# Linear attention with a token mixer: v loaded as bf16 by GpSimd-queue transfers, its products on VectorE, some relus on GpSimd

## The chip, the cores and the metric

The kernel runs on one core of one Trainium2 chip. A core has TensorE (PE, matrix products; PEld is its loading of weights), VectorE (DVE), ScalarE (ACT), GpSimd (POOL) and SyncE (SP, which here only issues transfers), and 16 DMA engines that move data between HBM and the on-chip memory. The metric is the device time of one execution in microseconds (us). Before the change the median of 2 runs is 120.28 us (120.14 to 120.42).

## What is computed

First cosine-weighted linear attention over batch 8, 8 heads, 576 positions, head size 64, then a token mixer over the 512 channels. All inputs and the output are fp32.

```python
theta = np.pi / 2.0 * pos / S
phi(x) = concatenate([relu(x) * cos(theta), relu(x) * sin(theta)])   # on the head axis
kv  = einsum('bhsf,bhsd->bhfd', phi(k), v)
z   = sum over s of phi(k)
num = einsum('bhsf,bhfd->bhsd', phi(q), kv)
den = einsum('bhsf,bhf->bhs', phi(q), z) + 1e-06
x   = num / den                                  # to (batch, seq, 512)
W_tok = scale * einsum('bsd,btd->bst', x @ w_q, x @ w_k)
mixed = einsum('bst,btd->bsd', W_tok, x)
out   = relu(mixed) @ w_out
```

## The kernel before, in words

The work on attention goes in 16 half batches H = 0 to 15: four heads each, that is two pairs of heads, and a pair's data is a tile of 128 partitions by 576 (a "part", a or b). A whole half batch of q, k or v is 128 x 1152. The second stage, the mixer, goes batch by batch, and the last products (WO) in 36 row tiles.

The order of all work is written out by hand in the string ORDER (lines 26 to 67). Each word is one step: a kind, a number, an optional part a or b, a PSUM place after a colon, and an engine after @ (A for ScalarE, V for VectorE, G for GpSimd). Line 555 runs through the words and issues each; every engine then takes its own instructions in just that order and waits for the semaphores that the data needs. So a step that waits holds up all that stands behind it on its engine. Transfers, too, wait in the queue of the engine that issues them until their buffer is free.

The steps that matter here:

- LQ, LK, LV (function load, line 142): transfers of q, k, v into fp32 buffers, one per part of 288 KB, all issued by SP (line 145). There are five buffers each of q, k and v (NRAW, line 101).
- RQ, RK (lines 222 to 227, helper relu at 201): relu of q and k into bf16, on ACT (line 203) or on DVE or POOL (line 205).
- CV (line 229): casts v to bf16 into one of two buffers vb; VS (line 232) then multiplies the bf16 v by the cosine and sine table vtab on DVE (line 234), which gives v2, twice as large.
- VG (line 239): the same product straight from the fp32 v, on POOL (line 248). Before the change the half batches 2a, 3, 4, 6, 7, 8, 13, 14 and 15 go this way; 0, 1, 2b, 5, 9, 10, 11 and 12 go by CV and VS.
- KV (line 268): PE products of k with v2 (lines 275 and 285), copied out of PSUM by KE.
- QT (line 290): PE transposes of q; QM (line 310) multiplies them by the q table on DVE (lines 316 and 320). N (line 329, matmuls at 340) is the product with kv; EP, RC and X divide by the denominator on ACT and DVE (X is line 393).
- XT, XR, XE, WK, KW, WQ, QW, KX, XK, XA, XB, MX, ME: transposes of x and the mixer. XA and XB, copies across partitions, are POOL's and ACT's.
- WO (line 504, matmuls at 509), OE (copy out of PSUM), ST (the stores, issued by SP at line 519, from 16 buffers).

At the start TK and TQ (lines 161 and 174) make index tables with iota on POOL; TV and TW turn them into sine and cosine on ACT.

Of the kernel before, what the change touches and what calls it, by code (L numbers as in the profile page):

```python
# [12 lines left out]
FP32 = mybir.dt.float32  # L13
BF16 = mybir.dt.bfloat16
# [17 lines left out]
XR1:0 RQ3a@A LQ5a X4 QT3:2 RK3@A LK4b VG4b QM3 XT2:6 LV5b XE1@A KV3:4 LV5a XE2@V RQ5b@A LK5a WK0:0
KE3@V RQ4@G LK5b KW0@A N6:4 CW0@A LV6b N7:6 VG4a EP6@A KX0:0 EP7@V RK4a@A LQ7a RJ3 X7 WQ0:1 RQ5a@A
LW2 QT4:2 X6 XK0@A LQ7b RK4b@A QM4 XT3:4 QW0@A CV5b@G LV6a KV4:0 XE3@A CV5a@G LK6b VS5 LV7a QT5:2
KE4@A WK1:4 XB0@A LK6a RK5@G N8:0 QM5 KW1@A N9:6 LQ6b EP8@A MX3:4 ME3@A LV7b VG6b KV5:2 RC8 EP9@V
XA0@A X8 LQ6a WQ1:4 RC9 KE5@A LK7b X9 RQ7@A N11:2 LK7a QW1@V N10:0 VG6a RC11 MX1:6 X11 KX1:4 LW4
ME1@A RC10 LW3 XK1@A MX0:2 X10 XT4:6 RK6b@A LW5 QT7:4 CW2@A XE4@V XA1@G XB1@A XR5:0 LQ8a RK6a@G
RQ6b@A QM7 MX6:6 ME6@A VG7a LQ8b KV6:4 ME0@A XE5@V LV8a MX5:6 MX7:2 RQ6a@V ME5@A LV9b WK2:0 ME7@A
KE6@V QT6:6 LV8b VG7b RK7@A KW2@V MX2:2 LQ9b MX4:4 QM6 KX2:1 LV9a ME4@A WQ2:0 ME2@A LV11a N12:4
CW3@V CW5@A N13:6 CW4@G LQ9a XK2@A KV7:2 EP13@V XA2@G RC12 RC13 X12 LK8a WO6:1 KE7@A QW2@A X13 VG8a  # L40
LK8b N14:4 OE6:0@A N15:2 LK9a EP14@V RQ8@A XR6:6 EP15@V RC14 WO1:1 X14 LV10a XB2@A RC15 WO4:0 LK9b
VG8b X15 CV9@A LV10b QT8:4 RQ9b@V WO7:2 OE4:1@V XE6@A WO3:3 QM8 RQ9a@G LV13b OE7:2@A LK11b MX9:6
MX11:4 ME9@A WO0:0 LQ10a VS9 LQ10b OE3:3@A MX10:6 LV11b ME11@A WO8:2 RK9a@G ME10@A LQ11a RK8@V QT9:4
OE8:4@A OE0:5@V RK9b@G LQ11b KV8:6 OE1:6@A QM9 KV9:2 CV10@G LQ13a KE8@A MX8:6 KE9@A N16:4 LK12a
ME8@A XR7:0 EP16@V RC16 N18:2 VS10 XE7@A WO12:6 LK11a WO10:7 LK10a X16 OE12:7@A LK10b WK3:6 OE10:8@V
CV11@G LV12a N17:4 KW3@A EP18@V N19:0 EP17@V LV12b WQ3:6 EP19@V RC17 RJ9 RK11b@G KX3:7 X17 LQ12a
QW3@A RQ10@A RQ11@G WO11:6 X19 X18 XT8:4 OE11:9@A LQ15b QT10:0 LQ14b VS11a XE8@A XT9:2 LQ12b QM10
WO5:6 RK10a@G LQ13b XE9@A LK13b QT11:0 VS11b XK3@A WO2:4 LK14b XB3@A XA3@G QM11 OE5:10@A RK10b@G
WK4:7 LQ15a OE2:11@A MX14:0 KW4@A LV13a KV10:2 RK11a@V ME14@A CV12@V KV11:6 LK12b KE10@A VS12 ST6
MX13:2 MX12:0 ME13@A KX4:4 LK13a VG13b ME12@A WQ4:5 LV14a KE11@A N21:2 XK4@A N20:0 EP21@V MX15:6  # L50
LV14b WO9:4 EP20@V RC21 ME15@A RC20 X20 RQ13@G N23:6 OE9:12@A X21 N22:0 QW4@A WO14:4 RQ12@A EP22@V
RK12a@G RC22 EP23@V X22 WO13:5 XB4@G OE14:13@A RC23 VG13a X23 RK13b@A QT12:0 ST14 WO17:4 OE13:0@A
LV15a QM12 RK12b@A LQ14a XR10:6 LK14a OE17:14@A MX18:0 XR11:2 LK15b XE10@V XA4@G ME18@A KV12:4
RK13a@A XE11@V WO16:0 VG14 KE12@A MX19:2 QT13:4 OE16:13@V ME19@A MX16:6 WK5:1 QM13 ME16@A ST16
KV13:2 LV15b KW5@A LK15a MX17:0 N24:6 ME17@A ST5 KX5:4 EP24@V KE13@V RC24 N26:2 XK5@V N25:0 X24
EP26@A RQ15@A XB5@G WO20:4 RQ14@G RC26 EP25@V RC25 WO18:5 X25 RK14b@A RK14a@G X26 N27:6 OE18:13@A
XA5@G WQ5:0 RC27 ST18 VG15 X27 KV14:2 QW5@A ST9 OE20:15@A MX20:0 XR13:6 KE14@A XR12:4 ME20@A XE13@V
QT14:2 XE12@A WO21:0 QM14 QT15:6 OE21:10@A N28:4 MX22:2 QM15 ST21 EP28@A WO15:0 RK15@A ST0 WK6:1
# [12 lines left out]
def kernel(  # L71
# [10 lines left out]
    nc = tc.nc  # L82

    B, NH, S, D = q.shape
    DM = NH * D
    DH = moe_w_q.shape[1]
    P = 128
# [14 lines left out]
    XC = DM // 2  # L102
    EPS_PE = (1, 2, 4, 5, 10, 11, 12, 27)
# [38 lines left out]
    def load(nm, H, part):  # L142
        b, h = divmod(H, 2)
        for r in (0, 1) if part is None else (part,):
            nc.sync.dma_start(raw[nm][H % NRAW][:, r, :], src[nm][b][:, 2 * h + r, :])  # L145
# [83 lines left out]
    def CV(H, ps, eng, part):  # L229
        cast(eng, vb_b[H % NPREP].rearrange(flat)[:, part], raw["v"][H % NRAW][:, part])  # L230

    def VS(H, ps, eng, part):
        n = part.stop - part.start
        V.tensor_mul(  # L234
            v2_b[H % NV2][:, part, :, :, 0:D],
            vb_b[H % NPREP][:, part].unsqueeze(3).to_broadcast([P, n, C, 2, D]),
            vtab.unsqueeze(1).to_broadcast([P, n, C, 2, D]))

    def VG(H, ps, eng, part):
        n = part.stop - part.start  # L240
        dst = v2_b[H % NV2]
        s = raw["v"][H % NRAW].rearrange("p r (c d) -> p r c d", d=D)
# [356 lines left out]
```

## Time and profile before

| | |
|---|---|
| median of 2 runs | 120.28 us |
| the profiled execution | 120.89 us, of which its span (first to last instruction) 119.1 us |
| granted TensorE clock, mean | 0.996 |
| busy PE / DVE / ACT / POOL | 98.2 / 90.0 / 84.6 / 69.6 us |
| moved by the DMA engines | 39.38 MB, 331 GB/s over the span |
| read from HBM / written to it | 29.62 / 9.44 MB |

How to read it: the busy time of an engine is what its instructions took, without the issuing of transfers. The page cuts the span into 40 equal slices of 2.98 us and gives the busy share of each in tenths. The chain that ended last goes back from the last instruction, step by step, to what released it. A group of instructions is a line of the kernel, an engine, an operation and shapes, with its total busy time, the mean duration of one in ns, and the idle time of the engine before them with what ended it. SPq is the queue of transfers that SP issues.

### The profile page before, as it was taken

The page shows a single profiled execution, that of the slowest core. Times are in us where ns is not written, and L with a number is a line of the kernel's source. Part 1 is how long each engine was busy: PE and PEld are TensorE (multiplying, and loading weights), DVE is VectorE, ACT ScalarE, POOL GpSimd, SP SyncE. Part 2 cuts the span into 40 slices and gives each one's busy share as a digit, 9 for nine tenths or more (in the row PEclk, how much of TensorE's full clock was granted, in tenths as well). Part 3 has the DMA queues.
Part 4 walks back from the last instruction along what each step waited for, and adds up shares of the span by engine and source line. Part 5 has one row for each costly group of instructions (what it writes and reads, how often), then busy time and mean ns, then how long its engine had stood idle before and what let it go on. Part 6 is the DMA issues. An engine that isn't in the chain of part 4 may idle for free.

```text
span 119.1 us, 4899 instructions
## 1 busy us (share of the span) xinstructions
PE 98.2 (82%) x2077; PEld 67.3 (57%) x2077; DVE 90.0 (76%) x162; ACT 84.6 (71%) x146; POOL 69.6 (58%) x65
## 2 busy tenths in 40 slices
PE   0030699779889789998999999999999999979970
PEld 0020578658677577553767776566767774634420
DVE  2049789995899997899798995997897988644510
ACT  6932394887987969897766997887579777336150
POOL 7304368599679994998674339987999220020000
PEclk9999999999999999999999999999999999999998
DMA  3999999999999999999999999959844797649974
GB/s 97 345 382 406 395 390 359 390 363 378 352 396 391 390 388 387 370 390 368 368 361 394 336 329 372 385 149 369 262 154 155 299 396 296 244 188 396 357 308 175
DMA packets 20662, 39.38 MB, mean 331 GB/s; under 512 B 3232, under 2 KB 3232, under 8 KB 20640
## 3 DMA queue, kind: packets, MB, share of 16 engines
q1 hardware_dynamic: 20640, 39.07, 90.0%
q8 instruction: 16, 0.26, 0.9%
q14 instruction: 6, 0.05, 0.2%
HBM read 29.62 MB, written 9.44 MB: 328 GB/s over the span
## 4 chain that ended last, share of the span: by engine, by line
PE 49%; DVE 23%; DMA 14%; SPq 3%; issue 3%; ACT 3%; POOL 2%; DVEq 0%; ACTq 0%
PE ps L509 17%; DVE x L393 9%; PE ps L340 8%; DVE qm L316 7%; DMA kraw<-in_k_dram 5%; DMA vraw<-in_v_dram 5%; PE ps L285 5%; PE ps L275 5%; PE ps L489 4%; DMA out_dram<-o 4%; SPq L145 3%; PE ps L295 3%; PE ps L466 2%; PE ps L439 2%; PE ps L452 2%
## 5 line engine op out<-in xcount | busy, mean ns | idle before, releaser
L248 POOL TENSOR_TENSOR v<-vraw,vtab 128x1152 bf16<-128x1152 f32 (+1 forms) x15 | 40.6, 2718 | 7.8 <-DMA vraw<-in_v_dram 4.1
L509 PE MATMUL ps<-wow,mix 128*128 128x512 bf16 x144 | 34.6, 380 | 0.8 <-ACT o L209 0.8
L393 DVE TENSOR_TENSOR x<-ps,rec 128x640 bf16<-128x640 f32 x32 | 25.6, 817 | 0.7
L316 DVE TENSOR_TENSOR qm<-ps,qtab 128x1152 bf16<-128x1152 bf16 x24 | 17.0, 750 | 6.4 <-PE ps L295 6.0
L509 PEld LDWEIGHTS <-mix 128*128 128x128 bf16 x144 | 12.7, 98 | 14.6 <-issue 1.4
L209 ACT COPY o<-ps 128x512 f32<-128x512 f32 x25 | 14.5, 585 | 8.1 <-PE ps L509 6.0
L500 ACT ACTIVATE mix<-ps 128x576 bf16<-128x576 f32 x27 | 17.0, 654 | 3.9 <-PE ps L489 3.6
L340 PE MATMUL ps<-kvs,qm 64*128 64x65 bf16 x640 | 14.3, 193 | 1.1 <-ACT kvs L209 0.5
L340 PEld LDWEIGHTS <-qm 64*128 64x128 bf16 x640 | 12.5, 96 | 4.2 <-issue 3.3
L295 PE MATMUL ps<-ident,rq 128*128 128x128 bf16 x108 | 9.0, 235 | 6.6 <-ACT rq L203 6.5
L203 ACT ACTIVATE rk<-kraw 128x576 bf16<-128x576 f32 (+1 forms) x15 | 11.4, 776 | 2.9 <-DMA kraw<-in_k_dram 2.4
L205 POOL TENSOR_SCALAR rk<-kraw 128x576 bf16<-128x576 f32 (+1 forms) x10 | 10.0, 1007 | 5.3 <-DVE x L393 2.0
L211 POOL TENSOR_SCALAR kx<-kx 64x256 bf16<-64x256 bf16 x11 | 4.4, 399 | 14.3 <-ACT kx L209 13.8
L295 PEld LDWEIGHTS <-rq 128*128 128x128 bf16 x108 | 7.3, 105 | 8.3 <-ACT rq L203 6.5
L203 ACT ACTIVATE rq<-qraw 128x1152 bf16<-128x1152 f32 (+1 forms) x12 | 11.5, 961 | 0.2
L285 PE MATMUL ps<-v,rk 64*64 64x130 bf16 x360 | 7.3, 228 | 4.8 <-POOL rk L205 4.8
L209 ACT COPY xT<-ps 128x1280 bf16<-128x1280 bf16 (+1 forms) x9 | 10.6, 1179 | 0.6 <-PE ps L419 0.5
L234 DVE TENSOR_TENSOR v<-vb,vtab 128x2304 bf16<-128x2304 bf16 (+1 forms) x9 | 10.2, 1147 | 0.7 <-POOL vb L211 0.5
L213 DVE COPY o<-ps 128x512 f32<-128x512 f32 x11 | 7.6, 687 | 4.1 <-PE ps L509 4.0
L275 PE MATMUL ps<-v,rk 64*128 64x260 bf16 x108 | 8.1, 295 | 2.0 <-DVE qm L316 1.5
L205 POOL TENSOR_SCALAR rq<-qraw 128x1152 bf16<-128x1152 f32 (+1 forms) x7 | 6.6, 939 | 5.0 <-DMA qraw<-in_q_dram 4.8
L285 PEld LDWEIGHTS <-rk 64*64 64x64 bf16 x360 | 5.9, 112 | 5.7 <-POOL rk L205 5.0
(66 smaller groups left out, 139.8 us busy)
## 6 DMA issues: line engine op xcount, KB each, us to landing
qraw<-in_q_dram SPq DMA_DIRECT2D x32, 288.0 KB, 5.8
vraw<-in_v_dram SPq DMA_DIRECT2D x32, 288.0 KB, 5.8
kraw<-in_k_dram SPq DMA_DIRECT2D x32, 288.0 KB, 5.9
out_dram<-o SPq DMA_DIRECT2D x36, 256.0 KB, 2.9
wof<-in_moe_w_out_dram SPq DMA_DIRECT2D x4, 256.0 KB, 6.1
wkf<-in_moe_w_k_dram SPq DMA_DIRECT2D x1, 128.0 KB, 7.2
wqf<-in_moe_w_q_dram SPq DMA_DIRECT2D x1, 128.0 KB, 5.9
```

The lines of the kernel that those rows point to most:

```text
L203: A.activation(dst, s, AF.Relu)
L205: eng.tensor_scalar(dst, s, FMAX, 0.0, op0=ALU.min, op1=ALU.max)
L209: A.copy(dst, s)
L248: G.tensor_mul(dst[:, part, :, :, 0:D], s[:, part].unsqueeze(3).to_broadcast([P, n, C, 2, D]), vtab.unsqueeze(1).to_broadcast([P, n, C, 2, ...
L275: nc.tensor.matmul(kv_v[:, r, :], rk_b[H % NPREP][a, 2 * c * D:2 * (c + 1) * D], v2_b[H % NV2][a, :, c, :, 0:D + 1], start=(c == 0), stop= ...
L285: nc.tensor.matmul(kv_v[o, r, :], rk_of(H)[a, pr, c, :], v2_b[H % NV2][a, pr, c, :, 0:D + 1], start=(c == 0), stop=(c == C - 1))
L295: nc.tensor.transpose(qt_v[:, c, :], rq_b[H % NPREP][:, c, :, :], ident)
L316: V.tensor_mul(qm_b[H % NQM][:, :, r, 0:C, :], q_t[:, r].unsqueeze(1).to_broadcast([P, 2, C, H2]), qtab)
L340: nc.tensor.matmul(nv[:, pr, u, :], qm_b[H % NQM][a, s, r, 2 * u:2 * u + 2, :], kv_b[H % 2][a, r, pr if H in KV_WIDE else 0, s, 0:D + 1], ...
L393: V.tensor_tensor(x_b[b % NX][:, :, 4 * h:4 * h + 4, :].rearrange("p u (w r) d -> p r w u d", r=2)[:, r], nv[:, :, :, 0:D], rec(g).to_broa ...
L500: A.activation(dst, s, AF.Relu, scale=scale_moe)
L509: nc.tensor.matmul(o, mix_b[bp % 2][:, m, rt * P:(rt + 1) * P], wow[:, m, :], start=(m == 0), stop=(m == NDM - 1))
```

## The change

- For the half batches 2 to 15 (V_CONV) v is read by transfers that POOL issues on its own queue, from fp32 in HBM straight into bf16 buffers vb. There are now five of these (NVB) instead of two. The even half batches are read with one transfer of both parts, the odd ones part by part.
- Half batches 0 and 1 are read as before, into two fp32 buffers (NRV) instead of five.
- All products VG become VS: 13 of one part (2a, 3a, 3b, 4a, 4b, 6a, 6b, 7a, 7b, 8a, 8b, 13a, 13b) and two of both parts (14, 15) move from POOL to DVE. The casts CV2b, CV9 (ACT), CV5a, CV5b, CV10, CV11 (POOL) and CV12 (DVE) go.
- 15 relus move to POOL: from ACT RQ3a, RQ3b, RQ5a, RQ5b, RQ7, RQ15, RK3, RK7, RK13a, RK13b and RK15; from DVE RQ6a, RQ9b, RK8 and RK11a.
- The places of the other words in ORDER stay. The words LV now say when POOL issues the transfer. The first of them, LV2, stands between TI and TQ, at the place of the former LV2b.

The diff, without the ORDER string (only its first lines, as an example):

```diff
-LQ0a TB TZ LQ0b LV0b TK LV1a TI T2 LV0a TV LV2b TQ LQ1b LK1b LK0b TW LK0a RQ0@A LQ1a QT0:0 LV1b
-CV0a@A LQ2a QM0 LQ2b RQ1b@G LK1a CV1a@V LV2a CV0b@V VS0 RK0b@A LK2b LK2a RK0a@G CV2b@A LV3b RQ1a@G
+LQ0a TB TZ LQ0b LV0b TK LV1a TI T2 LV0a TV LV2 TQ LQ1b LK1b LK0b TW LK0a RQ0@A LQ1a QT0:0 LV1b
+CV0a@A LQ2a QM0 LQ2b RQ1b@G LK1a CV1a@V CV0b@V VS0 RK0b@A LK2b LK2a RK0a@G LV3b RQ1a@G KV0:0 CV1b@V
...
+    NVB = 5
+    NRV = 2
+    V_CONV = (2, 3, 4, 5, 6, 7, 8, 9, 10, 11, 12, 13, 14, 15)
...
-    raw = {nm: bufs(NRAW, [P, 2, HC], FP32, f"{nm}raw") for nm in "kqv"}
+    raw = {nm: bufs(NRV if nm == "v" else NRAW, [P, 2, HC], FP32, f"{nm}raw") for nm in "kqv"}
...
-    vb_b = bufs(NPREP, [P, 2, C, D], BF16, "vb")
+    vb_b = bufs(NVB, [P, 2, C, D], BF16, "vb")
...
     def load(nm, H, part):
         b, h = divmod(H, 2)
+        if nm == "v" and H in V_CONV:
+            ps = slice(0, 2) if part is None else slice(part, part + 1)
+            nc.gpsimd.dma_start(vb_b[H % NVB].rearrange("p r c d -> p r (c d)")[:, ps],
+                                src[nm][b][:, 2 * h + ps.start:2 * h + ps.stop, :])
+            return
         for r in (0, 1) if part is None else (part,):
-            nc.sync.dma_start(raw[nm][H % NRAW][:, r, :], src[nm][b][:, 2 * h + r, :])
+            nc.sync.dma_start(raw[nm][H % len(raw[nm])][:, r, :], src[nm][b][:, 2 * h + r, :])
...
     def VS(H, ps, eng, part):
         n = part.stop - part.start
         V.tensor_mul(
             v2_b[H % NV2][:, part, :, :, 0:D],
-            vb_b[H % NPREP][:, part].unsqueeze(3).to_broadcast([P, n, C, 2, D]),
+            vb_b[H % NVB][:, part].unsqueeze(3).to_broadcast([P, n, C, 2, D]),
             vtab.unsqueeze(1).to_broadcast([P, n, C, 2, D]))
```

More of the change, by code (lines that the diff above doesn't have):

```diff
@@ L32 @@
[L32 to L37, printed above, removed]
@@ new lines @@
+N9:6 LQ6b EP8@A MX3:4 ME3@A LV7b VS6b KV5:2 RC8 EP9@V XA0@A X8 LQ6a WQ1:4 RC9 KE5@A LK7b X9 RQ7@G
+N11:2 LK7a QW1@V N10:0 VS6a RC11 MX1:6 X11 KX1:4 LW4 ME1@A RC10 LW3 XK1@A MX0:2 X10 XT4:6 RK6b@A LW5
+QT7:4 CW2@A XE4@V XA1@G XB1@A XR5:0 LQ8a RK6a@G RQ6b@A QM7 MX6:6 ME6@A VS7a LQ8b KV6:4 ME0@A XE5@V
+LV8 MX5:6 MX7:2 RQ6a@G ME5@A LV9b WK2:0 ME7@A KE6@V QT6:6 VS7b RK7@G KW2@V MX2:2 LQ9b MX4:4 QM6
+KX2:1 LV9a ME4@A WQ2:0 ME2@A LV11a N12:4 CW3@V CW5@A N13:6 CW4@G LQ9a XK2@A KV7:2 EP13@V XA2@G RC12
+RC13 X12 LK8a WO6:1 KE7@A QW2@A X13 VS8a LK8b N14:4 OE6:0@A N15:2 LK9a EP14@V RQ8@A XR6:6 EP15@V
@@ new lines @@
+RC14 WO1:1 X14 LV10 XB2@A RC15 WO4:0 LK9b VS8b X15 QT8:4 RQ9b@G WO7:2 OE4:1@V XE6@A WO3:3 QM8 RQ9a@G
+LV13b OE7:2@A LK11b MX9:6 MX11:4 ME9@A WO0:0 LQ10a VS9 LQ10b OE3:3@A MX10:6 LV11b ME11@A WO8:2
+RK9a@G ME10@A LQ11a RK8@G QT9:4 OE8:4@A OE0:5@V RK9b@G LQ11b KV8:6 OE1:6@A QM9 KV9:2 LQ13a KE8@A
+MX8:6 KE9@A N16:4 LK12a ME8@A XR7:0 EP16@V RC16 N18:2 VS10 XE7@A WO12:6 LK11a WO10:7 LK10a X16
+OE12:7@A LK10b WK3:6 OE10:8@V LV12 N17:4 KW3@A EP18@V N19:0 EP17@V WQ3:6 EP19@V RC17 RJ9 RK11b@G
+KX3:7 X17 LQ12a QW3@A RQ10@A RQ11@G WO11:6 X19 X18 XT8:4 OE11:9@A LQ15b QT10:0 LQ14b VS11a XE8@A
@@ L229, in CV @@
     def CV(H, ps, eng, part):
-        cast(eng, vb_b[H % NPREP].rearrange(flat)[:, part], raw["v"][H % NRAW][:, part])
+        cast(eng, vb_b[H % NVB].rearrange(flat)[:, part], raw["v"][H % NRV][:, part])
     def VS(H, ps, eng, part):
@@ L241, in VG @@
         dst = v2_b[H % NV2]
-        s = raw["v"][H % NRAW].rearrange("p r (c d) -> p r c d", d=D)
+        s = raw["v"][H % NRV].rearrange("p r (c d) -> p r c d", d=D)
         if H in VG_SPLIT:
```

37 lines of the change are left out of this document (15 added, 22 removed).

## The prediction, made before the result was known

> **What bounds the kernel now.** I read the page first: the busy shares, then the 40 slices.
>
> ```profile
> span 119.1 us, 4899 instructions
> PE 98.2 (82%) x2077; PEld 67.3 (57%) x2077; DVE 90.0 (76%) x162; ACT 84.6 (71%) x146; POOL 69.6 (58%) x65
> PE   0030699779889789998999999999999999979970
> DVE  2049789995899997899798995997897988644510
> DMA  3999999999999999999999999959844797649974
> ```
>
> No engine is full over the whole span, but the slices show two regimes. Up to the sixteenth slice (about 48 us) PE has holes while DVE and the DMA engines are nearly full; after it PE is full almost to the end. The busy time by stage gives sizes:
>
> ```profile
> 12.00:32.00 20.00, 16.97 (x410) 14.05 (x412) 17.41 (x28) 14.75 (x26) 14.71 (x10) 1.00 1.05 376
> 32.00:44.00 12.00, 10.27 (x249) 8.38 (x245) 11.16 (x20) 9.91 (x19) 10.93 (x8) 1.00 1.05 388
> 44.00:60.00 16.00, 15.55 (x364) 9.96 (x361) 13.97 (x28) 14.05 (x25) 12.04 (x9) 1.00 1.04 375
> 60.00:80.00 20.00, 19.59 (x400) 13.27 (x400) 17.91 (x35) 16.39 (x29) 13.77 (x12) 1.00 0.93 337
> 80.00:100.00 20.00, 19.95 (x566) 13.80 (x558) 16.81 (x33) 15.70 (x29) 12.52 (x8) 1.00 0.77 275
> ```
>
> The columns after the stretch and its length are PE, PEld, DVE, ACT, POOL (busy us and instructions), the granted clock, the DMA share and GB/s. From 44 us to 100 us PE idles 0.45 + 0.41 + 0.05 = 0.9 us in 56. Whatever PE loses before 44 us is therefore lost for good, and a saving elsewhere after 44 us is worth nothing. Before 44 us, DVE idles only 20 - 17.41 = 2.59 us and 12 - 11.16 = 0.84 us. Last I read the chain that ended last, in the front:
>
> ```profile
> 5.23 5.93 DMA kraw<-in_k_dram
> ...
> 25.24 5.81 DMA vraw<-in_v_dram
> ...
> 31.13 0.67 POOL vb L211
> ...
> 31.83 0.68 POOL vb L211
> ...
> 32.53 1.36 DVE v L234
> 33.89 1.34 DVE qm L316 x2
> ...
> 35.28 1.20 PE ps L275 x18
> ```
>
> Two things bound the front: arriving loads (a k half at 11.2 us, a v half at 31 us), and behind them DVE, which hands its product straight to PE. The question is whether the change lightens the loads or burdens DVE.
>
> **The change part by part.** The durations:
>
> ```profile
> L248 POOL TENSOR_TENSOR v<-vraw,vtab 128x1152 bf16<-128x1152 f32 (+1 forms) x15 | 40.6, 2718 | 7.8 <-DMA vraw<-in_v_dram 4.1
> L234 DVE TENSOR_TENSOR v<-vb,vtab 128x2304 bf16<-128x2304 bf16 x6 | 8.1, 1346 | 0.7 <-POOL vb L211 0.5
> L234 DVE TENSOR_TENSOR v<-vb,vtab 128x1152 bf16<-128x1152 bf16 x3 | 2.2, 749 | 0.0
> L205 DVE TENSOR_SCALAR rq<-qraw 128x576 bf16<-128x576 f32 x2 | 1.5, 741 | 0.0
> L205 DVE TENSOR_SCALAR rk<-kraw 128x1152 bf16<-128x1152 f32 x1 | 1.2, 1220 | 0.0
> L205 DVE TENSOR_SCALAR rk<-kraw 128x576 bf16<-128x576 f32 x1 | 0.4, 448 | 0.0
> L213 DVE CAST vb<-vraw 128x1152 bf16<-128x1152 f32 x1 | 0.8, 751 | 0.0
> L205 POOL TENSOR_SCALAR rk<-kraw 128x1152 bf16<-128x1152 f32 x1 | 1.5, 1501 | 0.9 <-ACT kvs L209 0.9
> L205 POOL TENSOR_SCALAR rk<-kraw 128x576 bf16<-128x576 f32 x9 | 8.5, 952 | 4.4 <-DVE x L393 2.0 <-DMA kraw<-in_k_dram 1.6 <-PE ps L489 0.5
> L205 POOL TENSOR_SCALAR rq<-qraw 128x1152 bf16<-128x1152 f32 x4 | 4.6, 1145 | 0.1
> L205 POOL TENSOR_SCALAR rq<-qraw 128x576 bf16<-128x576 f32 x3 | 2.0, 665 | 4.9 <-DMA qraw<-in_q_dram 4.8
> ```
>
> DVE. The 15 fp32 products of POOL (13 half parts, 2 whole) become bf16 products on DVE: 13 x 0.749 + 2 x 1.346 = 12.43 us. What leaves DVE: two q relus 1.48, k relus 1.22 and 0.45, one cast 0.75, together 3.90 us. Net +8.5 us, from 90.0 to 98.5.
>
> POOL loses 40.6 us of products and four casts (two halves of 0.67 and 0.68 in the chain above, two whole ones of at least twice that: some 4 us), and takes 15 relus: six q halves at 0.665, two whole q at 1.145, four whole k at 1.501, three k halves at 0.952, together 15.1 us. Of its 69.6 us about 40 are left, and 21 transfer issues come (seven whole, fourteen half). ACT loses eleven relus and two casts. I cost that at nothing on the path: after 44 us PE is full and can't gain, and before it the chain above has no relu of ACT in it. If ACT were what holds PE in the front, rival E would show it.
>
> Where the DVE work lands decides. The POOL products by stage:
>
> ```profile
> 12.00:32.00 20.00, 11.84 (x5) 1.00 1.05 376
> 32.00:44.00 12.00, 7.93 (x4) 1.00 1.05 388
> 44.00:60.00 16.00, 6.19 (x3) 1.00 1.04 375
> 60.00:80.00 20.00, 5.49 (x2) 1.00 0.93 337
> 80.00:100.00 20.00, 9.14 (x2) 1.00 0.77 275
> ```
>
> (One of the three in the third row is carried over from the second.) The written order keeps each product at its place, so the new DVE products fall there too. Five in 12 to 32 us: +3.75. Four in 32 to 44: +3.00, less one q relu 0.74. So +6.0 us by 44 us, against 3.43 us of DVE idle. In 44 to 60 us: +1.50 - 0.74 - 1.22 = -0.46. In 60 to 80: +1.50 - 0.45 - 0.75 = +0.30 against 2.09 idle. In 80 to 100: two whole ones, +2.69 against 3.19 idle.
>
> How much of the early idle can the products fill? What it was:
>
> ```profile
> DVE rec L359 <- PE ps L340: 1.7, 4, 0.9
> DVE vb L213 <- DMA vraw<-in_v_dram: 0.9, 1, 0.9
> DVE v L234 <- POOL vb L211: 0.5, 1, 0.5
> ```
>
> If all is filled, the excess is 6.0 - 3.43 = 2.6 us; if none, 6.0. The 0.5 behind POOL's cast is fillable, since that cast goes. The 0.9 stands ahead of the first new product, so it isn't. The waits on PE sit in a loop in which PE itself waits for DVE's x and qm, so they move along with it. I take half: 6.0 - 1.7 = +4.3 us on PE by 44 us. DVE's relief of 0.46 after that lets PE regain at most the 0.45 us that it idles there: -0.4. The late 2.7 us I cost at nothing, because PE there never waits for DVE; if that cover (DVE's lead) is gone, they cost up to 2.7.
>
> The first load. The whole of half batch 2 is now issued from POOL ahead of the iota of the q table, while only one half of it stood in SP's stream ahead of the k half that ends at 11.2 us. The sync queue has one 288 KB transfer less ahead of that k half and the other queue two more: 0.295 MB at 376 GB/s is 0.78 us. It is -0.8 if the new queue has moved nothing by then, +0.8 if it has moved all; I take +0.4. The iota's delay holds ACT's table and the first q relu, but DVE then still waits for loads. Later loads keep their total bytes read from HBM, so I take no gain from the narrower writes.
>
> The issue itself. No POOL transfer is in the trace; the nearest rows are SP's issues and the landing:
>
> ```profile
> L145 SPq DMA_DIRECT2D vraw<-in_v_dram x32: 327/332/1236, 1.6 to 83.0; - x32
> DMA to landing us min/median/max: 3.4/5.8/7.2
> ```
>
> Between 0.33 us and 5.8 us of POOL time each. In 12 to 44 us POOL idles 32 - 14.71 - 10.93 = 6.4 us, loses 19.8 us of products and 1.4 of casts, and takes five q halves, one whole q, one whole k, 6.0 us; that frees 21.5 us for some ten issues, so an issue is hidden up to 2.1 us. I take about 1 us, as it is SP's kind of work nearer to the low end, and so nothing on the path. Each issue also waits until the product five half batches earlier has read its bf16 buffer; behind it on POOL stand the relus and the kx copies. With the issues placed some two half batches ahead of their use that product is long done, and I cost the wait at nothing; without that cover it is rival B. SP loses 28 issues of 0.33 us, so q and k go out earlier, but at a DMA share of 1.05 up to 60 us they only share full engines: nothing, unless the front is bound otherwise. The Trainium skill, page "DMA: Bandwidth & Descriptors", section "Latency and other measured facts", puts the first byte of this kind of transfer at about 1 us, the emission overhead of GpSimd's cores; by it the sum stays as it is. No run here shows it yet.
>
> Sum: +4.3 - 0.4 + 0.4 = +4.3, bounds 2.6 - 0.8 - 0.4 = +1.4 and 6.0 + 0.8 + 2.7 = +9.5. The profiled execution took 120.89 us (span 119.1 and 1.8 around it), 0.6 above the median of 120.28; the difference is the same on both, so 125.2 for a profiled run and 120.28 + 4.3, about 124.5, for the median.
>
> One contention on the way. A DVE product beside POOL relus in the timeline:
>
> ```profile
> 54.20 1.35 DVE L234 TENSOR_TENSOR v<-vb,vtab 128x2304 bf16<-128x2304 bf16 x1
> 54.18 3.02 POOL L205 TENSOR_SCALAR rk<-kraw 128x576 bf16<-128x576 f32 x2 [0.54 <-PE ps L489]
> ```
>
> DVE took its usual 1.35 us though POOL had started 0.02 us before; the two relus took 1.5 us each instead of the 0.67 that such a half takes undisturbed. So I charge POOL, which has room, and not DVE. The Trainium skill, page "SBUF — State Buffer", section "Who interferes with whom", says that a DVE instruction with two SBUF inputs and a GpSimd one that reads SBUF exclude each other, and that the later one is blocked until the first is done. Here the later one was not; the trace disagrees in this pair.
>
> **The rivals.** B, late v: POOL's queue is in order, and v5 to v15 now stand behind relus that themselves wait for raw loads; or a converting transfer moves more slowly. It decides above 2.1 us per issue. At 3 us, ten issues cost 9 us by 44 us, which lie beside the DVE excess and not on top of it: about +9, 129. For it: the loads are what the front waits for. Against it: five bf16 buffers of v, so most issues run ahead.
>
> C, the lock: a new DVE product that meets one of the relus now on POOL waits for its end. With 17 half parts' worth and some 0.9 us a meeting, five meetings before 44 us cost 4.5 us more than forecast: 129. Against it stands the pair above. (The rule of the Trainium skill's page "SBUF — State Buffer" would do this here.)
>
> D, absorbed: all idle of DVE takes up products, and the first k half comes earlier: 2.6 - 0.8 - 0.4 = +1.4, of which the removed casts can give back all (0.67 + 0.68 us in the chain). Between 0 and +1.4, say +0.7: 121.0.
>
> E, the other side: the front belongs to the loads alone. A converted v5 that needn't queue in SP's stream lands 3.4 us after 25.24 at best, at 28.6, and no cast follows, so its product may start up to 3.9 us before 32.53. PE idles 3.03 + 1.73 = 4.8 us in 12 to 44; with 3 us of that gone, 117.3. It decides if DVE reaches that product before about 30 us with five products more in its queue. Against: DVE waited only 0.5 us for that product's input (the whole L234 row), so it came to it at 32.0 already.
>
> **How the numbers follow.** A (forecast, DVE overloaded in the front) 0.43, own range 122.5 to 127; B 0.17; C 0.05; D 0.20, from 118.5 to 122.4; E 0.15. Two per cent of 120.28 is 2.4 us, about what a measurement of this kernel can tell from no change. So faster 0.15 (E), same 0.20 (D), slower 0.65 (A, B, C). The range of 118.0 to 130.0 leaves out most of E and the far part of B, less than 0.2.
>
> **What would show it.** Right: 24 DVE products at L234's successor at 0.75 and 1.35 us; DVE near 98 us busy and without idle from 16 to 44 us; PE idle of 12 to 44 us grown from 4.8 to about 9, its waits there naming DVE x and qm; and PE full afterwards. Wrong: POOL waits naming transfers, or PE waits on v behind a DMA (B); DVE products above 0.75 us (C); PE idle below 4.8 us in the front (E); DVE still idling 2 us or more there with no shift (D). If a POOL issue shows more than 2 us, or the DMA rate falls below 370 GB/s in 12 to 44 us, the step on the issue is the one that failed.

## The result and the profile after

The changed kernel took 129.34 us (median of 2 runs, 128.52 and 130.17) against 120.28 us before: the ratio is 1.072, 95% interval 1.066 to 1.079. It is slower, as forecast, but by about twice the 4.3 us of the sum. The profiled execution took 128.52 us, 7.6 us more than the 120.89 us of the kernel before, and its span grew by the same 7.6 us, from 119.1 to 126.7 us. It is the faster of the two: the medians lie 9.1 us apart, and what follows accounts for the 7.6 us alone. The comparisons here and below leave disturbed executions out, so a ratio need not be that of two medians. In the changed kernel the line numbers from the loads on are 7 higher than before: L234 is now L241, L205 is L212, and the transfers of v that POOL issues are L148.

From the page of the changed kernel, the busy times and the slices (now of 3.17 us each):

```profile
span 126.7 us, 4870 instructions
PE 97.8 (77%) x2065; PEld 67.5 (53%) x2077; DVE 98.2 (77%) x172; ACT 74.7 (59%) x133; POOL 52.8 (42%) x82
PE   0030697667898667998999999969997998997980
DVE  2028699999998999899789977989997978754520
DMA  4999999999999999999980398999544299487884
```

PE and PEld do the same work as before. DVE has the 98.2 us that were forecast (98.5), partly by luck, since its products are 2.3 us longer than charged (below). POOL and ACT are far from full; unlike the figures before the change, POOL's 52.8 us contain the 13.4 us of its issues, and the other 39.4 are the 40 that were forecast. The holes of PE reach to the sixteenth slice, now about 51 us, and two show later, in the twenty-seventh and the thirty-first, where it was full before. The stages, with the columns of the prediction:

```profile
12.00:32.00 20.00, 14.68 (x376) 12.23 (x378) 18.21 (x30) 9.71 (x17) 12.06 (x16) 1.00 1.09 344
32.00:44.00 12.00, 9.75 (x214) 7.67 (x211) 11.30 (x20) 8.12 (x17) 3.65 (x6) 1.00 1.09 342
44.00:60.00 16.00, 13.56 (x277) 9.13 (x276) 15.41 (x29) 9.94 (x18) 10.56 (x16) 1.00 1.09 315
60.00:80.00 20.00, 19.31 (x448) 13.62 (x448) 16.55 (x30) 16.24 (x29) 10.80 (x12) 1.00 0.73 205
80.00:100.00 20.00, 17.76 (x461) 11.88 (x465) 18.51 (x33) 12.59 (x23) 9.04 (x12) 1.00 0.69 194
```

PE's idle time in these stages is 5.32, 2.25, 2.44, 0.69 and 2.24 us; before it was 3.03, 1.73, 0.45, 0.41 and 0.05. The largest growth is in 12 to 32 and 44 to 60 us, and then, where the prediction saw a full PE, in 80 to 100 us. What PE waited for from 12 to 50 us in the changed kernel (first rows of the waits; the POOL wait of 4.5 us ahead of them has a twin in the kernel before), and behind it the two largest waits for DVE in the kernel before:

```profile
PE ps L282 <- DVE qm L323: 1.7, 2, 1.0
PE ps L496 <- DVE x L400: 1.4, 2, 0.9
PE ps L347 <- DVE kvs L220: 1.4, 2, 0.7
PE ps L555 <- DVE x L400: 1.0, 1, 1.0
PE ps L413 <- DVE x L400: 0.9, 2, 0.6
```

```profile
PE ps L275 <- DVE qm L316: 1.5, 2, 1.0
PE ps L406 <- DVE x L393: 0.5, 1, 0.5
```

All of it names DVE, and what grew are the waits for x and for kvs (the KV products copied out of PSUM); the wait for qm is hardly longer than before. The products on DVE by shape, the issues on POOL, and the times from issue to landing:

```profile
L241 DVE TENSOR_TENSOR v<-vb,vtab 128x1152 bf16<-128x1152 bf16 x16 | 13.2, 826 | 0.9 <-DMA vb<-in_v_dram 0.9
L241 DVE TENSOR_TENSOR v<-vb,vtab 128x2304 bf16<-128x2304 bf16 x8 | 11.9, 1487 | 1.2 <-PE ps L292 1.1
L148 POOL DMA_DIRECT2D vb<-in_v_dram x21 | 13.4, 639 | 1.8 <-DVE v L241 1.7
```

```profile
qraw<-in_q_dram SPq DMA_DIRECT2D x32, 288.0 KB, 7.4
kraw<-in_k_dram SPq DMA_DIRECT2D x32, 288.0 KB, 7.6
vb<-in_v_dram POOLq DMA_DIRECT2D x7, 288.0 KB, 8.1
vb<-in_v_dram POOLq DMA_DIRECT2D x14, 144.0 KB, 7.2
```

The means are 826 and 1487 ns instead of 749 and 1346: in all 25.1 us instead of 16 x 0.749 + 8 x 1.346 = 22.75. An issue on POOL takes 0.64 us, within the 2.1 us that are hidden. The q and k transfers, untouched by the change, take 7.4 and 7.6 us to land instead of the 5.8 and 5.9 us of before.

To see where the delay arises, I follow one event per half batch: the start of its KV matmuls on PE. The rows of one line's KV matmuls from 40 us on, in the kernel before and in the changed one, begin with half batch 7:

```profile
L285 PE MATMUL ps<-v,rk x108: 215/217/242, 47.0 to 58.3; 64*64 64x130 bf16 x108
```

```profile
L292 PE MATMUL ps<-v,rk x108: 215/217/243, 52.0 to 63.4; 64*64 64x130 bf16 x108
```

It starts 5.0 us later (47.0 and 52.0). All shifts, in us against the kernel before, read from the first weight load of each KV step in the two traces; the last column is that of the last WO step:

```
half batch        0     3     5     7     8    11    12    15   last WO
before, at      12.4  25.7  35.0  47.0  57.2        80.1  94.1  114.2
changed kernel  +0.8  +2.4  +2.5  +5.0  +5.1  +5.3  +6.2  +7.2  +7.6
```

So 0.8 us is lost ahead of the first KV step, 4.2 us from there to 47 us, next to nothing from 52 to 75 us, and 2.3 us after that.

The chain that ended last tells another story than the waits. Its shares by engine, in the kernel before and in the changed one:

```profile
PE 49%; DVE 23%; DMA 14%; SPq 3%; issue 3%; ACT 3%; POOL 2%; DVEq 0%; ACTq 0%
DMA 39%; PE 30%; DVE 18%; SPq 4%; ACT 4%; issue 3%; POOL 0%; POOLq 0%; DVEq 0%; ACTq 0%
```

From 4.6 to 42.5 us the new chain consists almost wholly of loads of k, q and weights. By it alone the transfers would be the cause. But the share is a poor witness: in e9 below, with every transfer as before and the front within 0.2 us of before, DMA has 40% too. Only the experiments can decide. In the late part the chain runs through a transfer of v (half batch 13) and the product behind it; the second of these fences is POOL's timeline at that place:

```profile
73.65 0.41 POOL kx L218
...
74.74 8.12 DMA vb<-in_v_dram
82.86 0.02 issue
82.89 0.76 DVE v L241
```

```profile
73.64 0.40 POOL L218 TENSOR_SCALAR kx<-kx 64x256 bf16<-64x256 bf16 x1 [6.39 <-ACT kx L216]
74.13 0.67 POOL L212 TENSOR_SCALAR rk<-kraw 128x576 bf16<-128x576 f32 x1
74.74 0.60 POOL L148 DMA_DIRECT2D vb<-in_v_dram  x1
```

POOL waits 6.39 us for ACT's kx before a copy, and the issue of the transfer stands behind that copy and a relu in POOL's order.

### The profile page after: what moved, and what is told of

Same layout as the page of the kernel before. It is cut to its first block, busy times and chain, and to the rows that moved or that the text cites. A ratio compares the mean times of both kernels' runs of the same rounds, so it can differ in the third digit from the quotient of the medians.

```text
span 126.7 us, 4870 instructions
## 1 busy us (share of the span) xinstructions
PE 97.8 (77%) x2065; PEld 67.5 (53%) x2077; DVE 98.2 (77%) x172; ACT 74.7 (59%) x133; POOL 52.8 (42%) x82
## 2 busy tenths in 40 slices
DMA packets 20550, 35.25 MB, mean 278 GB/s; under 512 B 3120, under 2 KB 6704, under 8 KB 20528
## 3 DMA queue, kind: packets, MB, share of 16 engines
q0 software_dynamic: 3920, 4.13, 19.7%
## 4 chain that ended last, share of the span: by engine, by line
DMA 39%; PE 30%; DVE 18%; SPq 4%; ACT 4%; issue 3%; POOL 0%; POOLq 0%; DVEq 0%; ACTq 0%
PE ps L516 15%; DMA kraw<-in_k_dram 13%; DMA wqf<-in_moe_w_q_dram 6%; DMA vb<-in_v_dram 6%; DMA qraw<-in_q_dram 5%; DVE x L400 5%; DMA wof<-in_moe_w_out_dram 5%; DVE v L241 4%; SPq L152 4%; DMA out_dram<-o 4%; DVE qm L323 3%; PE ps L347 3%; PE ps L496 2%; PE ps L473 2%; PE ps L292 2%
## 5 line engine op out<-in xcount | busy, mean ns | idle before, releaser
L516 PE MATMUL ps<-wow,mix 128*128 128x512 bf16 x132 | 33.3, 380 | 2.3 <-ACT o L216 0.8
L241 DVE TENSOR_TENSOR v<-vb,vtab 128x1152 bf16<-128x1152 bf16 (+1 forms) x24 | 24.9, 1046 | 2.1 <-PE ps L292 1.1
L212 POOL TENSOR_SCALAR rk<-kraw 128x576 bf16<-128x576 f32 (+1 forms) x17 | 17.1, 1014 | 11.0 <-DMA kraw<-in_k_dram 6.5
L212 POOL TENSOR_SCALAR rq<-qraw 128x576 bf16<-128x576 f32 (+1 forms) x15 | 14.6, 979 | 14.6 <-DMA qraw<-in_q_dram 4.2
L148 POOL DMA_DIRECT2D vb<-in_v_dram x21 | 13.4, 639 | 1.8 <-DVE v L241 1.7
L496 PE MATMUL ps<-wq,kx 64*128 64x288 bf16 x64 | 8.1, 287 | 2.4 <-DVE x L400 1.4
L210 ACT ACTIVATE rk<-kraw 128x576 bf16<-128x576 f32 x10 | 6.6, 678 | 3.2 <-DMA kraw<-in_k_dram 3.2
```

What stands on the lines that cost most here:

```text
L148: nc.gpsimd.dma_start(vb_b[H % NVB].rearrange("p r c d -> p r (c d)")[:, ps], src[nm][b][:, 2 * h + ps.start:2 * h + ps.stop, :])
L212: eng.tensor_scalar(dst, s, FMAX, 0.0, op0=ALU.min, op1=ALU.max)
L241: V.tensor_mul(v2_b[H % NV2][:, part, :, :, 0:D], vb_b[H % NVB][:, part].unsqueeze(3).to_broadcast([P, n, C, 2, D]), vtab.unsqueeze(1).to_ ...
L496: nc.tensor.matmul(pair(ps)[:, t, :].bitcast(FP32)[:, 0:HS], kx_b[b % 2][a, (m // 2) ^ t, (m % 2) * P:(m % 2 + 1) * P], wq_b[b % 2][a, :], ...
L516: nc.tensor.matmul(o, mix_b[bp % 2][:, m, rt * P:(rt + 1) * P], wow[:, m, :], start=(m == 0), stop=(m == NDM - 1))
```

## The experiments

Theory 1: DVE's added time is the loss, in the front (1a) and also in the late part, where the prediction costed it at nothing (1c). Theory 2: the transfers, later or slower than SP's. Theory 3: the lock, DVE products that wait for POOL. The runs with doubled or added DVE work write to a tile that nobody reads.

**e1, the transfers alone.** The changed transfers, with the 15 products left on POOL (reading vb) and the relus where they were.

```diff
-        s = raw["v"][H % NRAW].rearrange("p r (c d) -> p r c d", d=D)
+        s = vb_b[H % NVB]
```

> Of the change only the converting GpSimd-queue transfers of v and the dropped casts stay; the 15 moved products go back to POOL (reading the bf16 v) and all relus to their engines of before. Theory 1 (the products on DVE cost the 7.6 us of the span): within 1.5 us of before, about 120.5, what is left being the later first k half (+0.8). Theory 2 (the transfers cost it: late, behind waiting steps on POOL's queue, slower to land): 125 to 129, since all transfers are as in the changed kernel.

129.51 us, ratio 1.073 (1.065 to 1.082). It looks like theory 2, but the run isn't clean. DVE's own nine products took 15.1 us instead of the 10.3 us (8.1 + 2.2) of the kernel before:

```profile
L241 DVE TENSOR_TENSOR v<-vb,vtab 128x2304 bf16<-128x2304 bf16 (+1 forms) x9 | 15.1, 1681 | 0.8 <-PE ps L292 0.7
```

With POOL's products waiting for other things than before, they now run beside DVE's, and one holds up the other. The loss can't be given to the transfers.

**e2, the DVE load alone, as products.** The kernel before, with a second bf16 product on DVE behind each of POOL's 15, four relus of DVE on POOL as in the change.

```diff
+        V.tensor_mul(
+            dx_o[:, part].rearrange("p r c t d -> p (r c t) d"),
+            dx_i.unsqueeze(1).to_broadcast([P, 2 * n * C, D]),
+            vtab[:, 0, 0].unsqueeze(1).to_broadcast([P, 2 * n * C, D]))
```

> The kernel before with all its transfers, casts and POOL products, and at each of the 15 moved products' places one more bf16 product of the same size on DVE, whose result nobody reads; the four relus that the change takes from DVE go to POOL as in the change, the cast CV12 stays: +9.3 us of DVE work. Theory 1: 124 to 128, PE's new holes before 46 us and again after 80. Theory 2: within 1.5 us of before.

137.82 us, ratio 1.132 (1.120 to 1.144): a loss of 17 us where 3 to 7 were expected. The 15 products should take 12.4 us; they took 26.0. The group, and a pair from the timelines of DVE and of POOL:

```profile
L246 DVE TENSOR_TENSOR dxo<-dxi,vtab 128x1152 bf16<-128x1152 bf16 (+1 forms) x15 | 26.0, 1734 | 0.0
```

```profile
16.46 2.64 DVE L246 TENSOR_TENSOR dxo<-dxi,vtab 128x1152 bf16<-128x1152 bf16 x1
```

```profile
16.12 2.37 POOL L260 TENSOR_TENSOR v<-vraw,vtab 128x1152 bf16<-128x1152 f32 x1 [3.06 <-DMA vraw<-in_v_dram]
```

POOL's product ends at 18.49; DVE's, begun at 16.46 and 0.75 us long, ends at 19.10, some 0.6 us after. It got through only when the other had ended. The 24 qm products, which take one of their inputs from PSUM, kept their mean of 750 ns in the same run; it is the products with both inputs in SBUF, the large on-chip memory, that are held up. The lock exists, and the run measures it rather than DVE's time.

**e3, late v issued early.** The changed kernel, with four words of ORDER moved ahead.

```diff
-LV13a ... LV14 ... LV15a ... LV15b     (each at its place)
+LV12 LV13a LV14 LV15a LV15b            (behind LV12)
```

> The changed kernel with only the issues of v13a, v14, v15a and v15b moved up on POOL's queue, behind that of v12, so that they no longer stand behind the kx copies and the relus. If late v makes the second loss (KV12 to the end, some 2.6 us in the span): 2 us less than the changed kernel, about 126.5. If DVE's whole products of v14 and v15 make it: no change, within 0.5 us of the changed kernel.

127.3 us, ratio 1.057 (1.048 to 1.065); the span is 125.7 us, 1.0 below that of the changed kernel. The late transfer on the chain is worth about 1 us, between the two expectations: behind half batch 11, 1.1 us are lost instead of 2.3.

**e4, the first v late.** The changed kernel, with LV2 behind the loads of half batch 1 and q of half batch 2.

```diff
-TI T2 LV0a TV LV2 TQ ... LQ2b RQ1b@G LK1a
+TI T2 LV0a TV TQ ... LQ2b RQ1b@G LV2 LK1a
```

> The changed kernel with only the issue of v2 moved behind the first relu on POOL (RQ1b), so that it no longer goes ahead of the first k half. If the first k half comes 1.2 us later because v2 is ahead of it: it lands at about 11.2 us again, the first product starts 0.8 us earlier, and the end comes 0.8 us earlier if nothing later bounds. If the loads behind decide: no change. In both cases v2a's product, needed at about 16 us, should still be in time.

129.59 us, ratio 1.071 (1.061 to 1.081). The first KV step starts as before (+0.04 us instead of +0.8), but that of half batch 2 comes 2.25 us late instead, for want of v2 (DVE waits 2.31 us for its landing). The 0.8 us are real and can't be had this way.

**e5, DVE's time without the lock.** The kernel before, transfers and POOL products as they were; each of the 15 products is followed on DVE by a memset of the length of its bf16 product (it reads nothing), and four relus go from DVE to POOL. The cast of v12 stays on DVE, so 9.3 us are added and not the 8.5 of the change.

```diff
+    def DX(H, ps, eng, part):
+        V.memset(dx_o[:, 0:829 if part.stop - part.start == 1 else 1546], 1.0)
```

> The kernel before with, at the places of the 15 moved products, memsets on DVE of about the same length (829 or 1546 bf16 elements) that read nothing, and the four DVE relus on POOL as in the change. Theory 1a (DVE's time alone makes the front's loss): KV7 starts about 4 us later than before and the end is at about 125. Theory 1b (much of it is that DVE and POOL exclude each other when both read the on-chip memory, as the doubled products beside POOL's own let it look): DVE instructions keep their length and the loss is under 5 us against the 17 of the doubled products. Theory 2 (the transfers): no loss, 120 to 121.5.

127.01 us, ratio 1.051 (1.046 to 1.057). The memsets took what they should:

```profile
L243 DVE MEMSET dxo<- 128x829 bf16 (+1 forms) x15 | 12.4, 829 | 2.2 <-issue 0.3
```

Nine of the 15 lay beside a POOL product for their whole length and took no longer than the others. With no transfer changed and no product stretched, 5.1 of the 7.2 per cent are there. The KV step of half batch 7 comes 4.2 us late and that of half batch 15 7.3 us.

**e6, everything but DVE's time.** The changed kernel with the 15 moved products cut to one column block of nine (eight ninths of these products are left out).

```diff
+            v2_b[H % NV2][:, part, 0:1, :, 0:D],
+            vb_b[H % NVB][:, part, 0:1].unsqueeze(3).to_broadcast([P, n, 1, 2, D]),
+            vtab[:, 0:1].unsqueeze(1).to_broadcast([P, n, 1, 2, D]))
```

> The changed kernel with the 15 moved products cut to one of their nine columns blocks (the other eight keep older values), so that DVE is relieved by some 11 us while every transfer, wait and relu stays. Theory 1: the front's loss goes, KV7 starts within 1 us of before, and the end is at 120 to 122. Theory 2: KV7 still 4 us late and the end at 126 to 129.

123.24 us, ratio 1.019 (1.014 to 1.023). Transfers and moved relus alone lose about 0.019 x 120.8 = 2.3 us, and taking away the time of DVE's products gives back 5.3 of the 7.2 per cent. The KV step of half batch 7 is 1.8 us late instead of 5.0, and 1.05 us are lost behind half batch 11 instead of 2.3. The chain that ended last has the place:

```profile
25.57 0.40 POOL vb L148
25.98 7.49 DMA vb<-in_v_dram
33.56 1.36 DVE v L241
```

This is v5, whose product went ahead at 32.53 before. It lands at 33.47; in the kernel before it landed at 31.05 and lost the time in two casts.

**e7, the queue alone.** The kernel before, with v (unconverted, from half batch 2 on) issued by POOL.

```diff
+            eng = nc.gpsimd if nm == "v" and H >= 2 else nc.sync
+            eng.dma_start(raw[nm][H % NRAW][:, r, :], src[nm][b][:, 2 * h + r, :])
```

> The kernel before with the v transfers of half batches 2 to 15 issued by POOL on its own queue at the same places, still fp32 and without conversion; casts, products and relus as before. If converting makes the transfers dearer (110 ns a row in the changed kernel, 93 to 103 for the rows of the sync queue): the rows here are near 100 ns, and DMA time is that of before. If the queue makes them so: 110 ns here too. The end: 120 to 122 if only conversion or DVE cost time; over 124 if issuing from POOL's in-order queue does.

128.11 us, ratio 1.061 (1.056 to 1.066). POOL, which still has its products, is busy for 86.0 us and the chain runs through them (17% of the span), so the time says little of the queue. Its rows say more: 28 halves of 288 KB land in 6.0 us, so POOL's queue as such isn't slow. SP's own q and k land in 7.6 and 6.6 us here, later than before, although nothing is converted. The queues of e7 and of the changed kernel (packets, MB, share of the 16 engines' span):

```profile
q0 software_dynamic: 2240, 8.26, 17.8%
```

```profile
q0 software_dynamic: 3920, 4.13, 19.7%
```

For the same 8.26 MB read, the engines work 0.197 x 126.7 = 25.0 us with the conversion and 0.178 x 126.5 = 22.5 us without: 11% more, though half as many bytes are written. The first line is that of e7 and the second that of the changed kernel, whose queue moves nearly twice as many packets, so the conversion and the smaller packets aren't separated; in e6, with the same transfers as the changed kernel, it is 0.199 x 121.6 = 24.2 us. A further run, e14 (v unconverted on POOL's queue, with the short products of e6), gave no result, so what the conversion alone does to the time stays open.

**e8, a few conversions.** The kernel before, with conversion for 5 and 9 to 12 alone, where casts go and no product moves.

```diff
+    V_CONV = (5, 9, 10, 11, 12)
```

> The kernel before with converting transfers only for the half batches whose v was cast anyway (5, 9, 10, 11, 12), so that six casts go (two halves and two wholes on POOL, one each on ACT and DVE) and no product moves; four fp32 and four bf16 buffers of v. Theory 1: as no DVE work is added and 0.75 us goes, the time is that of before or up to 1.5 us less (119 to 120.5). Theory 2: the five half batches arrive later than through the sync queue and it costs 1 to 3 us.

126.03 us over widely spread runs (123.54 to 127.11), no clear ratio: it decides nothing between the theories, and even the fastest run is no gain.

**e9 and e10, the memsets late and early.** As e5, with the memsets of 13, 14 and 15 alone (4.2 us of DVE's time; e9) or the other eleven alone (8.2 us; e10), and no relu moved.

```diff
-VG13b ... VG13a ... VG14 ... VG15
+VG13b DX13b ... VG13a DX13a ... VG14 DX14 ... VG15 DX15     (e9)
-VG2a ... VG3b ... VG8b
+VG2a DX2a ... VG3b DX3b ... VG8b DX8b                       (e10)
```

> The kernel before with memsets on DVE at the places of the last four moved products only (13b, 13a, 14, 15: 4.2 us), everything else as before. Theory 1c (the late products cost by themselves, the cover that the prediction counted on isn't there): the span grows by 2 to 2.7 us as it did after KV11 in the kernel with all fifteen memsets, so about 123. Theory 1d (they cost only because the front had already eaten DVE's lead): 120.5 to 121.3.

123.03 us, ratio 1.017 (1.012 to 1.022).

> The kernel before with the memsets on DVE at the places of the first eleven moved products only (2a to 8b, 8.2 us; no relu moved), everything else as before. KV7 starts 4 to 5 us late as with all fifteen. Theory 1c: the loss stays at that, about 125. Theory 1d: the same; it differs only in the run with the late ones alone. If the two runs' losses don't add up to the 6 us of all fifteen, the two stages aren't independent.

126.21 us, ratio 1.047 (1.039 to 1.055); the KV step of half batch 7 is 4.3 us late, and from half batch 8 (+5.3) to 11 (+5.2) nothing is added. The stage of 80 to 100 us of e9, and its waits on PE from 76 to 100 us:

```profile
80.00:100.00 20.00, 18.13 (x543) 13.04 (x543) 17.87 (x32) 13.73 (x26) 12.62 (x9) 1.00 0.64 224
```

```profile
PE ps L424 <- DVE x L398: 1.3, 1, 1.3
PE ps L494 <- DVE qm L321: 0.8, 1, 0.8
```

PE idles 1.87 us there instead of 0.05, and waits for DVE. Nothing but DVE's time was added, so theory 1c holds: DVE has no lead in the late part. The kernel before shows it already. There DVE's last product x of half batch 13 (X27) ends at 88.38 + 0.82 = 89.20 us, and PE begins to load x as weights at 89.26, and no idle time of PE gives it away:

```profile
88.38 0.82 DVE L393 TENSOR_TENSOR x<-ps,rec 128x640 bf16<-128x640 f32 x1
89.26 0.72 PEld L419 LDWEIGHTS <-x 64*128 64x128 bf16 x40
```

**e11 and e12, DVE relieved.** e11 is the changed kernel with 14 copies and casts of DVE (KE, XE, QW, KW, CW, XK) moved to ACT. e12 adds v2 through SP as before and 13 to 15 issued early.

```diff
-KE2@V XE2@V KE3@V QW1@V XE4@V ... XE10@V XE11@V KE13@V XK5@V XE13@V
+KE2@A XE2@A KE3@A QW1@A XE4@A ... XE10@A XE11@A KE13@A XK5@A XE13@A
```

> The changed kernel with 14 of DVE's copies out of PSUM and one weight cast given to ACT, which the change had relieved: nine of them before 50 us (5.8 us of DVE), five after 80 (3.3 us); nothing is left out. If DVE's time is what the change costs, KV7 starts only some 1.5 us later than before and the end is at 122 to 124. If ACT becomes late instead, or the transfers hold it, it stays over 126.

128.66 us, ratio 1.061 (1.051 to 1.070).

> The kernel of e11 with two more things: v2 is loaded and cast as before (no transfer ahead of the first k half), and v13a, v14, v15a, v15b are issued behind v12. If the start (0.8 us) and late v (1 us) add to DVE's part, it is 1.5 us under e11, 120.5 to 122.5; under 119 would beat the kernel before.

127.21 us, ratio 1.054 (1.047 to 1.061). Both missed their expectations. The front gained up to half batch 5 (+1.0 and +1.5 us instead of +2.5; in e12 1.7 us stand at half batch 1 already, behind the cast of v2 that e15 will show), but at half batch 6 the shift is +4.7 and +4.4: from about 15 to 45 us the chain of e12 is made of k and q transfers, and behind them of ACT. Whether it is the loads or the fuller ACT that takes the gain back wasn't separated.

**e13, e15 and e16, the places of the transfers.** e13 is e6 with both transfers of v5 issued ahead of the k relu behind which they stood. e15 mends three places in e6: v5 as in e13, v2 through SP at its old places (with both its casts on ACT), the last v early. e16 has the same mends with the full products.

```diff
-RQ3a@G LQ5a X4 QT3:2 RK3@G LK4b VH4b QM3 XT2:6 LV5b XE1@A KV3:4 LV5a
+RQ3a@G LV5b LV5a LQ5a X4 QT3:2 RK3@G LK4b VH4b QM3 XT2:6 XE1@A KV3:4
```

> As the run with short products (it leaves out eight of nine column blocks of the 15 moved products), but both v transfers of half batch 5 are issued from GpSimd ahead of the k relu of half batch 3 instead of behind it. In the run with short products that relu began at 24.31 us after GpSimd had waited 2.88 us for the k load, the v transfer behind it landed at 33.47 us, and DVE's product, which went ahead at 32.53 us in the kernel before, began at 33.56; the KV step of half batch 7 came 1.8 us late. Theory W (an in-order queue: the transfer waits behind a relu that waits for a load): the transfers go out at about 21.5 us, land by 30.5, the KV shift of half batch 7 falls from 1.8 to about 0.8 us, and the time from 123.2 to about 122.2 us. Rival X (traffic: v that goes ahead of k and q costs them what it gains): KV 3 to KV 5 come 0.5 to 1.5 us later than in the run with short products, and the time stays at 123 us or above.

Ratio 1.014 (1.007 to 1.021) against 1.019 (1.014 to 1.023) for e6: the intervals overlap, and neither theory W nor X is decided by the time. W's sign didn't come: in the one execution that was profiled (123.98 us) the KV step of half batch 7 is 3.0 us late, not 0.8. v5 no longer ends the chain; the next transfer, v6, does (issued at 28.8, landing 8.40 us later).

> As the run with short products (it leaves out eight of nine column blocks of the 15 moved products), with three places of the transfers mended: v of half batch 2 goes through the sync queue at its old places, with casts on ACT; v of half batch 5 is issued ahead of the k relu of half batch 3; the last halves and wholes of 13, 14 and 15 are issued some steps early. Theory W: these three places are all that the transfers cost, so the time is within 0.7 us of the kernel before (120.8) and no KV step comes more than 0.8 us late. Rival R (every converting row is dearer, and so every load lands later): the time stays 1.5 us or more above the kernel before, with the KV shift growing steadily from half batch 3 to 8.

122.12 us, ratio 1.012 (1.008 to 1.015). Between the two expectations: the mends win about 0.7 per cent, and 1.4 us stay. They aren't the price of the transfers, though. The KV step of half batch 0 is in time, but that of half batch 1 is already 1.5 us late, because the mend of v2 puts a cast on ACT that waits for its load, ahead of the relus of k:

```profile
16.02 0.67 ACT L216 CAST vb<-vraw 128x576 bf16<-128x576 f32 x1 [0.86 <-DMA vraw<-in_v_dram]
16.60 1.25 ACT L210 ACTIVATE rk<-kraw 128x576 bf16<-128x576 f32 x2
```

Before, these relus began at 15.02. From there the shift rises to 2.4 us at half batch 7 and falls back to 1.9 at half batch 8 and 1.4 at the last WO step. The steady growth that rival R named doesn't come. The chain shows v6 again:

```profile
26.71 1.78 POOL rq L212 x2
28.48 8.55 DMA vb<-in_v_dram
37.05 0.75 DVE v L248
```

> The changed kernel in full, with the three mended places of the transfers. Theory: what is left is DVE's own time, so about what the memsets on DVE cost alone: ratio about 1.05, 127 us, against 129 for the changed kernel; with the KV shift of half batch 7 at about 4.2 instead of 5.0 us. If loads and DVE's excess lie beside each other and not on top, the mends gain less than 1 us: 128 us or above. If the transfers were the larger part after all, it falls below 125 us.

126.86 us, ratio 1.051 (1.047 to 1.055), as expected. Of the changed kernel's 7.2 per cent the mends give back 2.1, and what is left equals the 5.1 of e5, which has none of the changed transfers. The cast of v2 delays half batch 1 here too, by 1.2 us, and yet the front is at +4.1 us at half batch 7, as in e10, which has no such cast: the delay lies beside DVE's excess and not on top of it. The last KV step is at +5.7. Between e15 and e16, which differ in the length of DVE's 15 products alone, lie 3.9 per cent.

No version tried that computes the reference's outputs is faster than the kernel before.

## Why the prediction was right in its cause and wrong in its size

- **What bounds the kernel: right.** DVE's time is the larger part of the loss: alone it costs 5.1 per cent (e5), and without it the changed kernel loses 1.9 instead of 7.2 (e6). The tell-tale signs came: 24 products on DVE, 98.2 us busy, PE's waits on x and qm (though those on x and kvs are the ones that grew), PE's idle time in 12 to 44 us grown from 4.8 to 7.6 us (not to 9); DVE idles 1.0 us of 16 to 44 us (2.6 before).
- **The front term, +4.3: right, within what was measured.** From the first KV step to that of half batch 7 it is 4.2 us in the changed kernel, 4.1 in e16 without the late transfers, 4.2 in e10 and 3.9 in e5. (In e5 and e10 the granted clock was 0.91 in 12 to 32 us, so a part of theirs may be the clock's; in e16 it was 1.00 there, but 1.2 us of it stand behind the cast of v2.) With short products 1.0 us is left of it (e6), so the transfers cost something in the front as well, but the two don't add up. DVE filled 29.51 - 28.57 = 0.94 us more of 12 to 44 us, and 1.6 us more of 16 to 44 us, behind the late first load, about the 1.7 that I took.
- **The late 2.7 us at nothing: the step that failed.** "PE there never waits for DVE" was read from a PE that was full, and that says nothing about the lead of the engine that feeds it. It had none: in the kernel before x is ready 0.06 us before PE loads it, e9 alone costs 1.7 per cent and opens 1.9 us of idle time on PE, and in the changed kernel 2.3 us are lost after half batch 11. The sentence behind it, "if that cover (DVE's lead) is gone, they cost up to 2.7", was the price. DVE's idle time of 3.19 us in that stage was no room, since it lay at the wrong places.
- **-0.4 regained in 44 to 60 us: wrong.** PE's idle time there grew from 0.45 to 2.44 us, in part because the front's own idle time now falls into that stage (39 to 55 us had 1.35 before). The shift stays at 5.0 to 5.3 from half batch 7 to 11, with nothing given back.
- **The first k half, +0.4: the bound of +0.8 came, partly by luck.** The k half lands at 12.37 us instead of 11.16, 1.2 us later and beyond the bound, but the relu behind it takes 0.67 us instead of 1.10. So the first KV step is 0.8 us late; it is in time with v2 out of the way (e4).
- **The issue, hidden up to 2.1 us: right in the price, wrong in the cover.** 0.64 us each. But the wait of the queue's other work was costed at nothing, and two issues stood behind it: v13 behind the kx copy (about 1 us, e3), v5 behind a relu in e6. This is rival B in small; at 1 to 2.6 us (e3, and the 2.1 per cent of e16) it is not the 9 us that I gave it, and the issue's own length was not what decided. That B and C had named 129 us, the time that came, is chance: the mechanism of neither made it.
- **"Later loads keep their total bytes read from HBM, so I take no gain from the narrower writes": there was none, and the engines had more work.** The changed transfers take 11% more of them than those of e7. SP's loads land later too, but that comes with the second queue, since they do so in e7 without any conversion. No run shows a price in time for it: the 1.4 us of e15 stand behind a cast on ACT, and with the full products nothing of it shows (e16). The sign that I had named for it, a DMA rate below 370 GB/s in 12 to 44 us, came (344 and 342) but tells nothing: the rate counts the bytes written, and those of a converted v are half as many (35.25 MB moved instead of 39.38).
- **The lock: my reading of one pair was wrong as a rule.** I charged POOL and not DVE, since one product beside two relus took its usual 1.35 us. In e2 a DVE product with both inputs in SBUF waits for POOL's product, and in the changed kernel, beside POOL's relus, the 24 products are 2.3 us longer in all. The Trainium skill, page "SBUF — State Buffer", section "Who interferes with whom", says that the later of two such instructions is blocked until the first is done; e2 agrees (2.64 us for a product of 0.75, ended 0.6 us after POOL's). In the pair of the prediction POOL had begun 0.02 us before and yet it was POOL that waited: the 1.5 us are the mean of 1.89 and 1.17, and the first relu ended 0.52 us after DVE's product. So who waits isn't settled by starts so close in the records. As a price of its own rival C didn't show all the same: e5, without any stretch, loses as much as e16, with 3.0 us of it (25.7 us of products).

The sum as it should have been: front +4.2, late +2.3, first half +0.8, and 0.3 in the rest: 7.6 us, the growth of the span. All of these were among the bounds (up to +9.5); it was the values taken within them that were low, and low in the same direction.

The sum is that of the profiled execution; the further 1.5 us between the medians, which rest on two runs each, aren't accounted for.

What stays open: how much of the 2.3 us of the late part is DVE's time and how much v13's transfer. Without DVE's time 1.05 us of it stay (e6), without the late transfer 1.1 (e3), which makes about half each; but e9 gives 1.5 us of span for DVE's time alone, and e5 loses 2.4 us there with no transfer changed. e9 and e10 together lose 6.4 per cent and e5, which has both and moves four relus away, 5.1. And why e11 and e12 gain nothing after 40 us was only read from the chain.

## What to carry to other kernels

That an engine at the end of the chain never waits for a feeder shows only that the feeder is in time, not by how much: before costing added work at nothing there, look for the feeder's lead at each product (its end against the start of the reader), and not for its idle time over a stage. A transfer that moves to a queue in order on a computing engine inherits every wait of that engine's other work. And to test an engine's time alone, use an instruction that reads nothing, since a copy of the real work brings its contention along.

## What the runs showed of the hardware

- A DVE product with both inputs in SBUF, 0.75 us alone, took 2.64 us beside a POOL product (e2), while products with one input in PSUM kept their 0.75 us; memsets of the same length beside the same POOL products took 0.75 and 1.35 us, unchanged (e5).
- Transfers that convert fp32 to bf16 wrote half the bytes, in nearly twice as many packets (3920 and 2240), and took 11% more of the transfer engines than those that don't (25.0 against 22.5 us of all 16 for 8.26 MB read). Issued by POOL, an unconverted half landed in 6.0 us and a converted one in 7.2.
- An issue on POOL took 0.54 to 0.90 us of its time, 0.64 in the mean, where SP's took 0.33.
- With transfers in a second queue, those of the first landed later though none of them changed: q from 5.8 to 7.4 us in the median, and to 7.6 in e7, where nothing was converted.
